# Spreading the first units' reciprocals with TensorE, taking the first block pair by pair, and zero products in planned gaps, in a fused attention and two-layer kernel

## The chip, the cores and the metric

The kernel runs on one core of a Trainium2 chip. The metric is the device time of one execution in microseconds (us).

## What is computed

Causal-by-block attention over 4 batches and 8 heads of 576 tokens with 64 columns, then two dense layers of 512 to 2048 to 512 with a nonlinearity in the middle of each. All of it is float32, on 2304 tokens.

```python
scores = scale * q @ k.T, masked where block_i < block_j (blocks of 64)
attn = exp(scores - max); attn = attn / (sum(attn) + 1e-9); x = attn @ v
h = x @ w_in;  g = h if h >= 1, 0 if h <= -1, else (h + 1) ** 2 / 4;  x = g @ w_out
h = x @ w_in2; g = max(0.01 * h, h);                                  out = g @ w_out2
```

## The kernel before

**Who orders the work.** The code builds a list of operations, each with an engine, a planned cost in ns, a priority and what it reads and writes (`Plan.op`, line 163). `Plan.schedule` (line 276) plays that list on a model of the engines forward and backward with random shifts (`SEED, TRIES = 13, 42`, line 64), keeps the order that ends first, and issues every engine's instructions in it. On the chip each engine then works in that order, so an instruction that waits holds up all that stand behind it on its engine. The model takes `port=True` operations of VectorE and GpSimd one at a time.

**Attention.** A unit is a pair of heads and a part of the rows: part "a" has chunks 0 to 2 (320 rows), part "b" chunks 3 and 4 (256 rows). There are 16 pairs, so 32 units. `unit_scores` (line 516) loads q and k, scales q on GpSimd (line 547), zeroes the columns that pad a chunk to a multiple of 128 keys (line 606, GpSimd, six a unit in part "a", four in part "b"), and multiplies into a PSUM slot (line 586). `softmax` (line 472) takes the maximum (line 484, VectorE), the exponential with its sum (line 491, ScalarE), the sum plus 1e-9 (line 495), its reciprocal (line 497), and multiplies the probabilities by it on GpSimd (line 502, one instruction a chunk and head, so six in a unit "a"). `unit_values` (line 662) transposes the probabilities (line 680), copies them out of PSUM (lines 685 and 687), and multiplies by v (line 696); in the first four units, which are parts "a" of pairs 0 to 3, 256 of the 320 columns go into the first block's input `x[0]` and `x[1]` (lines 707 and 708, the high part and the rest), the other 64 through line 710 to DRAM (line 711, queue SP). The units live in five "rooms" of SBUF (line 510).

**PSUM.** Slots 0, 3, 1 and 2 are two banks each. For the first seven units the ring of slots is 0, 3, 1, 2, and from then on 0, 3, 1 (lines 1182 to 1184). Slot 2's banks 4 and 5 go to the first layer after that: block 0 has bank 4 alone, blocks 1 and on have 4 and 5 (lines 1185 and 1202).

**Weights.** `w_float` (line 414) turns the 64-bit words of 16 slices of the first matrix into a high and a low part: a load (line 430, SP), line 431 (ScalarE), line 432 (GpSimd), lines 434 and 439 (VectorE), line 442 (ScalarE), line 445 (VectorE or GpSimd by turns).

**First layer.** `h1_block` (line 744) takes 256 tokens a block, nine blocks. Each of eight pairs of slices has two halves of three times four products of 128x128 by 128x256 (line 756), one TensorE operation of the plan for each four, and wants the whole of `x[0]` or `x[1]`; then lines 762 and 766 (ScalarE) and 767 (VectorE) empty the bank. After the attention come the conversions of the other matrices, and the layers of line 1127 and line 943, which fill TensorE to the end.

**Start.** Ten products of a zero tile (line 466) run before the first scores, into slot 2.

Of the kernel before, what the change touches and what calls it, by code (L numbers as in the profile page):

```python
# [49 lines left out]

AHEAD = 45.0


# [9 lines left out]

SEED, TRIES = 13, 42

# [87 lines left out]
class Plan:  # L153
# [122 lines left out]
    def schedule(self):  # L276
# [19 lines left out]
        for o, start, end in zip(self.ops, *best[1:]):  # L296
            o.start, o.end = start, end

        for o in done:
            o.fn()  # L300

# [3 lines left out]
def fused_kernel(ctx, tc, qk, qk2, v, w1, w2, out):  # L305
# [44 lines left out]
    def pool(cols, prio, fn, r, w, fixed=161):  # L350
        plan.op("POOL", fixed + 0.95 * cols, prio, fn, r, w, fixed != 200)

# [27 lines left out]
    ps_d.evicts.append(ps_b)  # L380
    ps_c = psum("psr", "psr", "ps_c", (), ((2, True),), "right")
    ps_e = psum("psr", "psr", "ps_e", ("psr",), ((2, False),), "right")

# [6 lines left out]
    def slot(i):  # L390

        return Bank(plan, (2 * i, 2 * i + 1), lambda: slots[i], {1: ps_b, 2: ps_c}.get(i, ps_a))

# [20 lines left out]
    def w_float(prio, fc):  # L414
# [12 lines left out]
        def upper():  # L427
# [43 lines left out]

    def softmax(prio, tag, s, parts):


        n = sum(len(p[2]) for p in parts)
        nm, sm, rs = small("nm", f"nm{tag}"), small("sm", f"sm{tag}"), small("rs", f"rs{tag}")
        i = 0
# [10 lines left out]
        for c, _, heads, view, probs, pbufs in parts:  # L488
            keys = CH[c][2]
            for k in range(len(heads)):  # L490
# [3 lines left out]
                i += 1  # L494
        act(n, prio, lambda: nc.scalar.activation(rs.get()[:, 0:n], sm.get()[:, 0:n], AF.Copy, bias=1e-9), [sm], [rs], sb=True,
            extra=60)
        dve(8, prio, lambda: nc.vector.reciprocal(rs.get()[:, 0:n], rs.get()[:, 0:n]), [rs], [rs])
# [10 lines left out]
    PCOL = {0: 0, 1: 128, 2: 384, 3: 0, 4: 512}  # L508
    units = {}
    ROOMS = {0: {"p": [(P1, 0)], "v": (P2, 1536), "qk": (P2, 2560)},  # L510
             1: {"p": [(P2, 0)], "v": (P2, 2176), "qk": (P2, 3392)},
# [4 lines left out]
    def unit_scores(pair, part, prio, ring, room_):  # L516
# [16 lines left out]
        qk_room = qs, qo, nqk  # L533
        units[pair, part] = vt, pr, prob

# [64 lines left out]
        for c in ((0, 1, 2) if part == "a" else (3, 4)):  # L600
            keys = CH[c][2]
            a, b_ = PCOL[c] + keys, PCOL[c] + (keys + 127) // 128 * 128
            for hd in range(2):
                if a == b_:
                    continue
                pool(0, prio - 1, lambda a=a, b_=b_, hd=hd: nc.gpsimd.memset(prob(hd, a, b_), 0.0), [], [part_of(hd, a, b_)], fixed=200)

# [7 lines left out]
        for grp in groups:  # L615
# [3 lines left out]
            def f(grp=grp, s=s):  # L619
                for i, (c, o) in enumerate(grp):  # L620
# [4 lines left out]
                (c, o, (0, 1), lambda s=s, o=o, c=c: s.get()[:, :, o:o + CH[c][2]],  # L625
                 [probs(c, 0), probs(c, 1)], [pbuf(c, 0), pbuf(c, 1)]) for c, o in grp])
        if part == "b":
# [10 lines left out]
            for hd in range(2):  # L638
                if ss:
                    s = ss[hd]  # L640
                else:
                    s = slot(ring[0])

                    def f(hd=hd, s=s):
# [4 lines left out]
                    (4, 224, (hd,), lambda s=s: flat2(s)[:, 224:800].rearrange("p (h k) -> p h k", h=1),  # L649
                     [probs(4, hd)], [pbuf(4, hd)])])  # L650

# [10 lines left out]
    def unit_values(pair, part, prio, ring, evac):  # L662
        n = f"{part}{pair}"
        vt, pr, prob = units[pair, part]
        pts = []
        for i, blocks in enumerate(TILES[part]):
# [7 lines left out]
            def f(blocks=blocks, s=s):  # L674
                for hd in range(2):
                    o = 0
                    for c, j in blocks:
# [21 lines left out]
        pe(sum(x[3] for x in SUMS[part]) * 1.7 + 150, prio, f, [vt] + pts, [s])  # L699
        xp = P2.reg(turn("xp", (4032, 4352)), SA)  # L700
        b, kc = divmod(pair, NKC)
        c0 = b * S + (0 if part == "a" else SA)

        q0 = 256 if c0 == 0 else 0
        if q0:
# [487 lines left out]
    for i in range(NBLK):  # L1193
# [108 lines left out]
```

## Time and profile before

| | us |
|---|---|
| three runs, median (lowest to highest) | 947.88 (946.68 to 949.87) |
| the profiled execution, its own time | 946.55 |
| its span, first to last instruction | 944.8 |
| TensorE busy in the span (98%) | 924.5 |
| VectorE, ScalarE, GpSimd busy | 759.3, 537.9, 321.2 |

Read it from TensorE: it is busy for all but 20.3 us of the span, so what can go is looked for in the stretches in which it waits. In the rows of stretches the columns are the stretch, its length, the busy time of TensorE (PE), its weight loads (PEld), VectorE (DVE), ScalarE (ACT) and GpSimd (POOL) with the number of instructions, the granted clock of TensorE as a share of full, the DMA engines' share, and GB/s.

### The profile page before, as it was taken

How to read it: one execution, taken by the hardware profiler on the slowest of the kernel's cores; microseconds unless marked ns; L12 is line 12 of the kernel's file. 1: busy time of each engine (PE TensorE's matmuls, PEld its weight loads, DVE VectorE, ACT ScalarE, POOL GpSimd, SP SyncE). 2: the span in 40 equal slices, each digit the busy share in tenths (PEclk: the TensorE clock that was granted, in tenths of full speed). 3: DMA queues.
4: the chain of work that ended last, by engine and by line, in shares of the span. 5: the costliest groups of instructions: out<-in, count | busy, mean ns of one | idle time of the engine just before them, and what ended most of it. 6: DMA issues, size and time to landing. Idle time of an engine off the chain costs nothing.

```text
span 944.8 us, 19895 instructions
## 1 busy us (share of the span) xinstructions
PE 924.5 (98%) x7324; PEld 876.0 (93%) x7324; DVE 759.3 (80%) x1289; ACT 537.9 (57%) x1060; POOL 321.2 (34%) x626
## 2 busy tenths in 40 slices
PE   7799999999999999999999999999999999999998
PEld 5467888888889999999999999999999999999998
DVE  4988867877889765779979697678888899887967
ACT  5888777877879666663334343344535563333422
POOL 6997767677665831000000020236653000000000
PEclk8999999999999999999999999999999999999999
DMA  8767878895879789976434599978885983453433
GB/s 278 235 197 224 269 255 284 297 303 185 277 264 325 262 313 326 332 246 206 149 104 143 155 348 326 342 251 276 298 292 195 322 263 91 156 156 102 145 90 113
DMA packets 168130, 221.91 MB, mean 235 GB/s; under 512 B 10080, under 2 KB 141664, under 8 KB 168032
## 3 DMA queue, kind: packets, MB, share of 16 engines
q1 hardware_dynamic: 168032, 220.63, 72.0%
q8 instruction: 58, 0.95, 0.4%
q14 instruction: 40, 0.33, 0.1%
HBM read 139.85 MB, written 80.74 MB: 233 GB/s over the span
## 4 chain that ended last, share of the span: by engine, by line
PE 91%; DVE 3%; issue 1%; ACT 1%; DMA 1%; POOL 1%; SPq 0%; DVEq 0%; ACTq 0%
PE bank L1127 30%; PE bank L756 22%; PE bank L943 18%; PE bank L1066 6%; PE slot L680 5%; PE slot L696 5%; PE slot L586 2%; PE slot L590 2%; DMA w<-w 1%; ACT rp L491 1%; DVE ra L851 1%; POOL rp L502 1%; DVE ra L1086 0%; DVE rp L687 0%; DVE wraw L1115 0%
## 5 line engine op out<-in xcount | busy, mean ns | idle before, releaser
L756 PE MATMUL bank<-ra,w 128*128 128x256 f32 x1728 | 229.2, 286 | 1.0 <-DVE rg L767 1.0
L756 PEld LDWEIGHTS bank<-ra,w 128*128 128x128 f32 x1728 | 213.2, 189 | 10.1 <-issue 5.6
L943 PE MATMUL bank<-rp,w 128*128 128x288 f32 x1344 | 180.9, 296 | 0.2 <-DVE rp L883 0.2
L943 PEld LDWEIGHTS bank<-rp,w 128*128 128x128 f32 x1344 | 179.5, 189 | 0.9 <-DVE rp L883 0.4
L851 DVE TENSOR_TENSOR ra<-ra,bank 128x288 f32<-128x288 f32 (+2 forms) x280 | 126.3, 488 | 39.9 <-ACT ra L853 13.2
L1127 PE MATMUL bank<-w,rp 128*128 128x256 f32 x1014 | 148.6, 281 | 0.0
L1127 PEld LDWEIGHTS bank<-w,rp 128*128 128x128 f32 x1014 | 132.8, 188 | 0.0
L1112 ACT ACTIVATE rp<-ra 128x1024 fp32r<-128x1024 f32 (+1 forms) x48 | 47.3, 988 | 75.7 <-DVE ra L1086 71.4
L811 POOL TENSOR_TENSOR w<-w 128x128 f32<-128x128 f32 x128 | 65.6, 533 | 41.9 <-DVE w L807 40.5
L1127 PE MATMUL bank<-rp,w 128*128 128x256 f32 x508 | 76.8, 282 | 0.0
L947 ACT ACTIVATE ra<-ra 128x1152 f32<-128x1152 f32 x32 | 37.4, 1168 | 68.0 <-DVE ra L851 68.0
L767 DVE SCALAR_TENSOR_TENSOR rg<-bank,rg 128x512 f32<-128x512 f32 x72 | 49.3, 685 | 28.5 <-ACT rg L766 28.2
L1127 PEld LDWEIGHTS bank<-rp,w 128*128 128x128 f32 x508 | 67.5, 188 | 0.1
L762 ACT ACTIVATE rg<-bank 128x512 f32<-128x512 f32 x72 | 43.0, 598 | 33.0 <-PE bank L756 32.5
L878 POOL TENSOR_TENSOR xs<-xs,rp 128x576 f32<-128x576 f32 x1 | 1.5, 1500 | 175.3 <-DMA xs<-x2d 175.3
L1115 DVE TENSOR_TENSOR wraw<-ra,rp 128x1024 fp32r<-128x1024 f32 (+1 forms) x48 | 54.3, 1134 | 6.9 <-PE bank L1127 2.4
L1127 PE MATMUL bank<-w,wraw 128*128 128x256 f32 x294 | 58.7, 282 | 0.2 <-DVE wraw L1115 0.2
L1086 DVE TENSOR_TENSOR ra<-rp,ra 128x256 f32<-128x256 f32 (+2 forms) x102 | 44.4, 439 | 2.3
L1127 PE MATMUL bank<-rg,w 128*128 128x256 f32 x280 | 46.3, 282 | 0.0
L766 ACT ACTIVATE rg<-rg 128x512 f32<-128x512 f32 x72 | 45.5, 632 | 1.0
L1086 DVE TENSOR_TENSOR ra<-rp 128x512 f32<-128x512 f32 (+2 forms) x51 | 34.4, 676 | 14.5 <-DMA rp<-gd 13.5
L1127 PEld LDWEIGHTS bank<-w,wraw 128*128 128x128 f32 x294 | 45.0, 188 | 0.6 <-DVE wraw L1115 0.4
(170 smaller groups left out, 1840.4 us busy)
## 6 DMA issues: line engine op xcount, KB each, us to landing
rp<-gd SPq DMA_DIRECT2D x41, 512.0 KB, 4.2
wcd<-w SPq DMA_DIRECT2D x43, 448.0 KB, 5.2
gd<-ra SPq DMA_DIRECT2D x32, 576.0 KB, 4.6
gd<-rg SPq DMA_DIRECT2D x64, 256.0 KB, 4.0
w<-wcd SPq DMA_DIRECT2D x32, 512.0 KB, 6.8
w<-wcd SPq DMA_DIRECT2D x32, 384.0 KB, 6.2
w<-w SPq DMA_DIRECT2D x44, 256.0 KB, 5.2
w<-w SPq DMA_DIRECT2D x16, 512.0 KB, 4.7
```

Of the source, the lines that this page charges most:

```text
L680: nc.tensor.transpose(s.get()[:, hd, o:o + 128], prob(hd, a, a + 128), ident.get())
L696: nc.tensor.matmul(s.get()[64 * hd:64 * hd + 64, 0, q0:q0 + m], lhsT=vt.get()[:, j, 64 * hd:64 * hd + 64], rhs=pts[i].get()[:, hd, o:o + m ...
L756: nc.tensor.matmul(ps.get()[:, 256 - j * 256:512 - j * 256], lhsT=win(fc, c, kc), rhs=xt[x].get()[:, kc], start=(k == 0 and kc == 0 and j ...
L767: dve(512, pv, lambda ps=ps, gt=gt: nc.vector.scalar_tensor_tensor(gt.get(), ps.get(), 1.0, gt.get(), op0=ALU.max, op1=ALU.min), [ps, gt], ...
L811: plan.op("POOL", 430, prio, lambda o=o, a=a, b=b, op=op: nc.gpsimd.tensor_tensor(sl(o), sl(a), sl(b), op=op), [(fx, (a, a + 1)), (fx, (b, ...
L851: dve(cols, prio, lambda: nc.vector.tensor_tensor(out(o), out(a), P[b][1](), op=op), [P[b][0], (slots, (a, a + 1))], [(slots, (o, o + 1))])
L943: nc.tensor.matmul(ps.get()[:, 0:HALF], lhsT=wc(1, p, cw, li, 128 * kc, 128 * kc + 128), rhs=r.get()[:, cx, kc], start=(k == 0 and kc == 0 ...
L1066: nc.tensor.matmul(ps[t].get()[:, 0:n], lhsT=wc(z, p, cw, li, 128 * t, 128 * t + 128), rhs=x.get()[:, n * zi:n * zi + n], start=(p == 0 an ...
L1086: dve(cols, pv, lambda f=f: nc.vector.tensor_tensor(*f(), op=ALU.subtract), r, [(tt, w)], port=True)
L1112: act(4 * n, pv, lambda tt=tt, ht=ht: nc.scalar.activation(s_(ht, 0, 4), s_(tt, 0, 4), AF.Copy), [tt], [ht], sb=True)
L1115: dve(4 * n, pv, lambda tt=tt, ht=ht, lt=lt: nc.vector.tensor_tensor(s_(lt, 0, 4), s_(tt, 0, 4), bc(s_(ht, 0, 4)), op=ALU.subtract), [tt, ...
L1127: nc.tensor.matmul(ps.get()[:, 256 * t:256 * t + w], lhsT=b if wide else g, rhs=g if wide else b, start=(p == 0 and k == 0 and t == 0), st ...
```

## The change

Each of these is in the diff below, cut to its core. The four first units keep their probabilities unnormalised: their reciprocals go into a tile `late` of 128x6, TensorE spreads each column over 64 partitions by a product with the identity matrix (six products a unit, float32), ScalarE copies the 320 columns to SBUF, and VectorE multiplies the values by them. ScalarE and VectorE then make `x[0]` and `x[1]` from SBUF, not PSUM. The first two pairs of block 0 are planned as one operation of three products for each quarter of the input. Pads are zeroed only where a room changes part. Slot 2 is no longer in the attention's ring; its banks 4 and 5 go to the first layer from block 0 on. The ten zero products at the start write bank 4. Where the plan has TensorE idle over 600 ns before its 20,000th ns, zero products are issued there, one for each 213 ns of 0.7 of the gap. Planned costs and port flags are changed in a few places, and the order is searched with another seed and 260 tries, so the order of all instructions is a new one.

```diff
+LATE = 4
+EARLY = 2
...
-SEED, TRIES = 13, 42
+FILL_UNTIL, FILL_SHARE = 20000, 0.7
+
+SEED, TRIES = 15, 260
...
+        last = 0
         for o in done:
+            if o.eng == "PE":
+                if last and o.start < FILL_UNTIL and o.start - last > 600:
+                    for _ in range(int((o.start - last) * FILL_SHARE / 213)):
+                        self.fill()
+                last = o.end
             o.fn()
...
-    ps_c = psum("psr", "psr", "ps_c", (), ((2, True),), "right")
-    ps_e = psum("psr", "psr", "ps_e", ("psr",), ((2, False),), "right")
+    ps_e = psum("psr", "psr", "ps_e", (), ((2, False),), "right")
...
-            op0=ALU.logical_shift_left, op1=ALU.bitwise_or), [hs, sg], [dst])
+            op0=ALU.logical_shift_left, op1=ALU.bitwise_or), [hs, sg], [dst], port=True)
...
-            dve(512, prio, low, *rw)
+            dve(512, prio, low, *rw, port=True)
...
-    zp = slot(2)
+    zp = bank(4)
+
+    def zeros():
+        nc.tensor.matmul(zp.get()[:, 0:128], lhsT=wz.get(), rhs=wz.get(), start=True, stop=True)
+    plan.fill = zeros
     for i in range(N_WARM):
-        pe(427, -1000, lambda: nc.tensor.matmul(zp.get()[:, 0, 0:128], lhsT=wz.get(), rhs=wz.get(), start=True, stop=True), [wz], [zp])
+        pe(427, -1000, zeros, [wz], [zp])
...
+        act(n, prio, lambda: nc.scalar.activation(r(), sm.get()[:, 0:n], AF.Copy, bias=1e-9), [sm], mine, sb=True, extra=60)
+        dve(8, prio, lambda: nc.vector.reciprocal(r(), r()), mine, mine)
+        if late is not None:
+            return
...
+        late = pt(st, [128, 6], F32, "late", f"late{n}", 6) if len(units) < LATE else None
...
-                if a == b_:
+                if a == b_ or padded.get(room_) == part:
                     continue
...
+        padded[room_] = part
...
-            pe(2 * m * 0.95, prio, f, [*dict.fromkeys(pr), ident], [s])
+            pe(2 * m * 0.85, prio, f, [*dict.fromkeys(pr), ident], [s])
...
+        xp = P2.reg(turn("xp", (4032, 4352)), SA)
+        if late is not None:
+            def f():
+                for i, c in enumerate((0, 1, 2) if part == "a" else (3, 4)):
+                    r = CH[c][1]
+                    q = CH[c][0] - (0 if part == "a" else SA)
+                    for hd in range(2):
+                        nc.tensor.matmul(s.get()[64 * hd:64 * hd + 64, 1, q:q + r], lhsT=late.get()[0:r, 2 * i + hd:2 * i + hd + 1].to_broadcast([r, 64]),
+                                         rhs=ident.get()[0:r, 0:r], start=True, stop=True, skip_group_check=True)
+            pe(nq * 1.7 + 150, prio, f, [ident, late], [s])
+            act(nq, prio, lambda: nc.scalar.activation(xp.get()[:, 0:nq], s.get()[:, 1, 0:nq], AF.Copy), [s], [xp])
...
+        if late is not None:
+            dve(nq, prio, lambda: nc.vector.tensor_tensor(xp.get()[:, 0:nq], s.get()[:, 0, 0:nq], xp.get()[:, 0:nq], op=ALU.mult), [s, xp], [xp])
+            if q0:
+                x = XB[0]
+                act(q0, prio, lambda: nc.scalar.activation(x[0].get()[:, kc], xp.get()[:, 0:q0], AF.Copy), [xp], [(x[0], (kc, kc + 1))], sb=True)
+                dve(q0, prio, lambda: nc.vector.tensor_tensor(
+                    x[1].get()[:, kc], xp.get()[:, 0:q0], bc(x[0].get()[:, kc]), op=ALU.subtract), [xp, (x[0], (kc, kc + 1))],
+                    [(x[1], (kc, kc + 1))], port=True)
+            dma(128 * (nq - q0) * 4, prio, lambda: nc.sync.dma_start(x1d[:, kc, c0 + q0:c0 + nq], xp.get()[:, q0:nq]), [xp],
+                [(f"x1d{kc}", (c0 + q0, c0 + nq))])
+            return
...
-            for j in range(2):
+            for kc in range(NKC if i == 0 and p < EARLY else 0):
+                for j in range(2):
+                    def f(fc=2 * p + j, j=j, kc=kc, ps=ps):
+                        for k, (c, x) in enumerate(((0, 0), (1, 0), (0, 1))):
+                            nc.tensor.matmul(ps.get()[:, 256 - j * 256:512 - j * 256], lhsT=win(fc, c, kc),
+                                             rhs=xt[x].get()[:, kc], start=(k == 0 and kc == 0 and j == 0),
+                                             stop=(k == 2 and kc == NKC - 1), skip_group_check=True)
+                    pe(3 * 119.5, pr - 8 * (NKC - 1 - kc) + 0.01 * j, f, [(W[p], (j, j + 1)), (W[p], (2 + j, 3 + j))]
+                       + [(x, (kc, kc + 1)) for x in xt], [ps])
+            for j in range(0 if i == 0 and p < EARLY else 2):
...
-    ring.append(2)
     attention(seq[:7])
-    ring.remove(2)
-    hb = [4]
+    hb = [4, 5]
...
-        if i == 1:
-            hb = [4, 5]
```

## Rows read from the trace of the kernel before

**Rows 1.** Stretches: us, busy PE, PEld, DVE, ACT, POOL, then clock, DMA.
```profile
0.00:7.40 7.40, 6.35 (x44) 5.60 (x44) 1.54 (x6) 1.80 (x5) 3.34 (x27) 1.00 0.69 209
7.40:12.70 5.30, 0.03 (x2) 0.02 (x1) 3.85 (x10) 4.45 (x22) 2.30 (x4) 0.84 1.02 339
12.70:50.00 37.30, 31.51 (x219) 19.85 (x220) 30.95 (x67) 29.58 (x102) 34.07 (x78) 0.93 0.75 250
50.00:150.00 100.00, 95.95 (x780) 80.86 (x781) 83.24 (x160) 79.85 (x221) 76.90 (x160) 1.00 0.78 242
150.00:930.00 780.00, 779.64 (x6198) 759.23 (x6197) 630.60 (x1028) 419.09 (x709) 204.63 (x361) 1.00 0.73 236
930.00:944.80 14.80, 11.06 (x89) 10.50 (x88) 9.14 (x23) 3.11 (x6) 0.00 (x0) 1.00 0.16 55
```

**Rows 2.** TensorE in order of time: start, length, line, count, idle before.
```profile
1.05 4.00 PE L466 MATMUL slot<-wz 128*128 128x128 f32 x20 [1.05 <-DVE wz L463]
4.98 2.44 PE L586 MATMUL slot<-rp 64*128 64x64 f32 x24
12.71 1.44 PE L586 MATMUL slot<-w 64*128 64x64 f32 x8 [5.29 <-ACT rp L491]
14.08 3.18 PE L680 MATMUL slot<-ident,rp 128*128 128x128 f32 x12
17.19 1.13 PE L586 MATMUL slot<-w 64*128 64x320 f32 x4
...
23.23 1.41 PE L696 MATMUL slot<-rp,rp 128*64 128x320 f32 x12
...
39.17 1.31 PE L680 MATMUL slot<-ident,rp 128*128 128x128 f32 x10 [0.48 <-ACT rp L491]
...
49.87 1.21 PE L756 MATMUL bank<-ra,w 128*128 128x256 f32 x8
...
60.55 0.73 PE L756 MATMUL bank<-ra,w 128*128 128x256 f32 x4 [1.04 <-DVE rg L767]
...
65.60 0.82 PE L586 MATMUL slot<-rp 64*128 64x64 f32 x8
...
68.27 0.81 PE L586 MATMUL slot<-rp 64*128 64x320 f32 x4 [1.05 <-DVE rp L687]
```

**Rows 3.** ScalarE: unit 0's last exponential, a weight's first pass.
```profile
9.07 0.54 ACT L491 ACTIVATE rp<-slot,nma 128x320 f32<-128x320 f32 x1
...
10.56 0.66 ACT L431 ACTIVATE xs<-w 128x512 f32<-128x512 f32 x1 [0.85 <-DMA w<-w]
```

**Rows 4.** GpSimd: reciprocals times probabilities, units 0 and 3.
```profile
11.35 3.46 POOL L502 TENSOR_SCALAR rp<-rp,rsa 64x64 f32<-64x64 f32 x6
...
28.76 2.85 POOL L502 TENSOR_SCALAR rp<-rp,rsa 64x64 f32<-64x64 f32 x6 [1.11 <-DVE rsa L497]
```

**Rows 5.** One stretch of two microseconds, columns as in rows 1.
```profile
12.00:14.00 2.00, 1.28 (x8) 0.96 (x8) 0.81 (x2) 2.00 (x11) 2.00 (x5) 0.50 1.04 420
```

**Rows 6.** TensorE's waits, first 60 us: total, times, longest.
```profile
PE slot L586 <- ACT rp L491: 6.2, 3, 5.3
PE slot L680 <- POOL rp L502: 2.2, 3, 1.0
```

**Rows 7.** 30 to 50 us, columns as in rows 1.
```profile
30.00:50.00 20.00, 15.86 (x121) 9.73 (x118) 18.79 (x39) 16.82 (x53) 19.43 (x36) 1.00 0.72 229
```

**Rows 8.** Line 708 on VectorE: ns shortest, median, longest; first and last start.
```profile
L708 DVE TENSOR_TENSOR ra<-slot,ra x4: 416/424/425, 20.7 to 38.3; 128x256 fp32r<-128x256 f32 x4
```

**Rows 9.** Line 606, the pads, whole run, columns as in rows 8.
```profile
L606 POOL MEMSET rp<- x98: 144/152/156, 1.2 to 296.0; 128x64 f32 x98
L606 POOL MEMSET w<- x62: 142/152/159, 2.3 to 309.0; 128x64 f32 x62
```

**Rows 10.** Groups by line, first 60 us: count, busy us, mean ns.
```profile
L434 DVE SCALAR_TENSOR_TENSOR w<-w 128x512 int32<-128x512 int32 x10 | 8.2, 817 | 1.4 <-POOL w L432 1.4
```

**Rows 11.** Line 434 alone, columns as in rows 8.
```profile
L434 DVE SCALAR_TENSOR_TENSOR w<-w x10: 661/688/1170, 11.3 to 56.9; 128x512 int32<-128x512 int32 x10
```

More of the change, by code (lines that the diff above doesn't have):

```diff
@@ L350, in pool @@
     def pool(cols, prio, fn, r, w, fixed=161):
-        plan.op("POOL", fixed + 0.95 * cols, prio, fn, r, w, fixed != 200)
+        plan.op("POOL", fixed + 0.95 * cols, prio, fn, r, w, fixed != 86)
     def dma(nbytes, prio, fn, r, w):
@@ L390, in slot @@
     def slot(i):
-        return Bank(plan, (2 * i, 2 * i + 1), lambda: slots[i], {1: ps_b, 2: ps_c}.get(i, ps_a))
+        return Bank(plan, (2 * i, 2 * i + 1), lambda: slots[i], {1: ps_b}.get(i, ps_a))
     def bank(i):
@@ L463, in fused_kernel, with softmax @@
     dve(0, -100, lambda: nc.vector.memset(wz.get(), 0.0), [], [wz], fixed=200)
-    zp = slot(2)
+    zp = bank(4)
+    def zeros():
+        nc.tensor.matmul(zp.get()[:, 0:128], lhsT=wz.get(), rhs=wz.get(), start=True, stop=True)
+    plan.fill = zeros
     for i in range(N_WARM):
-        pe(427, -1000, lambda: nc.tensor.matmul(zp.get()[:, 0, 0:128], lhsT=wz.get(), rhs=wz.get(), start=True, stop=True), [wz], [zp])
+        pe(427, -1000, zeros, [wz], [zp])
     dummy = Buf(plan, "dummy", 1, lambda: const.tile([128, 8], F32, name="dummy"))
     act(8, -1000, lambda: nc.scalar.activation(dummy.get(), wz.get()[:, 0:8], AF.Exp), [wz], [dummy], extra=1280)
-    def softmax(prio, tag, s, parts):
+    def softmax(prio, tag, s, parts, late=None):
         n = sum(len(p[2]) for p in parts)
-        nm, sm, rs = small("nm", f"nm{tag}"), small("sm", f"sm{tag}"), small("rs", f"rs{tag}")
+        nm, sm = small("nm", f"nm{tag}"), small("sm", f"sm{tag}")
         i = 0
@@ L494, in softmax, with r @@
                 i += 1
-        act(n, prio, lambda: nc.scalar.activation(rs.get()[:, 0:n], sm.get()[:, 0:n], AF.Copy, bias=1e-9), [sm], [rs], sb=True,
-            extra=60)
-        dve(8, prio, lambda: nc.vector.reciprocal(rs.get()[:, 0:n], rs.get()[:, 0:n]), [rs], [rs])
+        e = 0
+        if late is not None:
+            e = 2 * parts[0][0] + parts[0][2][0]
+            e -= 6 * (e > 5)
+            rs = late
+        else:
+            rs = small("rs", f"rs{tag}")
+        mine = [(rs, (e, e + n))]
+        def r():
+            return rs.get()[:, e:e + n]
+        act(n, prio, lambda: nc.scalar.activation(r(), sm.get()[:, 0:n], AF.Copy, bias=1e-9), [sm], mine, sb=True, extra=60)
+        dve(8, prio, lambda: nc.vector.reciprocal(r(), r()), mine, mine)
+        if late is not None:
+            return
         i = 0
@@ L509, in fused_kernel @@
     units = {}
+    padded = {}
     ROOMS = {0: {"p": [(P1, 0)], "v": (P2, 1536), "qk": (P2, 2560)},
@@ L533, in unit_scores @@
         qk_room = qs, qo, nqk
-        units[pair, part] = vt, pr, prob
+        late = pt(st, [128, 6], F32, "late", f"late{n}", 6) if len(units) < LATE else None
+        units[pair, part] = vt, pr, prob, late
         q0, k0, nq, nk, nj = (SA, 0, SA, SA, 3) if part == "a" else (0, SB, SB, S, 5)
@@ L603, in unit_scores @@
             for hd in range(2):
-                if a == b_:
+                if a == b_ or padded.get(room_) == part:
                     continue
-                pool(0, prio - 1, lambda a=a, b_=b_, hd=hd: nc.gpsimd.memset(prob(hd, a, b_), 0.0), [], [part_of(hd, a, b_)], fixed=200)
+                pool(0, prio - 1, lambda a=a, b_=b_, hd=hd: nc.gpsimd.memset(prob(hd, a, b_), 0.0), [], [part_of(hd, a, b_)], fixed=86)
+        padded[room_] = part
         def pbuf(c, hd):
@@ L625, in unit_scores @@
                 (c, o, (0, 1), lambda s=s, o=o, c=c: s.get()[:, :, o:o + CH[c][2]],
-                 [probs(c, 0), probs(c, 1)], [pbuf(c, 0), pbuf(c, 1)]) for c, o in grp])
+                 [probs(c, 0), probs(c, 1)], [pbuf(c, 0), pbuf(c, 1)]) for c, o in grp], late)
         if part == "b":
@@ L649, in unit_scores @@
                     (4, 224, (hd,), lambda s=s: flat2(s)[:, 224:800].rearrange("p (h k) -> p h k", h=1),
-                     [probs(4, hd)], [pbuf(4, hd)])])
+                     [probs(4, hd)], [pbuf(4, hd)])], late)
     def flat2(s):
@@ L663, in unit_values @@
         n = f"{part}{pair}"
-        vt, pr, prob = units[pair, part]
+        vt, pr, prob, late = units[pair, part]
         pts = []
@@ L698, in f @@
                                      skip_group_check=True)
-        pe(sum(x[3] for x in SUMS[part]) * 1.7 + 150, prio, f, [vt] + pts, [s])
-        xp = P2.reg(turn("xp", (4032, 4352)), SA)
+        pe(sum(x[3] for x in SUMS[part]) * 1.7 + 230, prio, f, [vt] + pts, [s])
         b, kc = divmod(pair, NKC)
@@ L704, in unit_values @@
         q0 = 256 if c0 == 0 else 0
+        if late is not None:
+            dve(nq, prio, lambda: nc.vector.tensor_tensor(xp.get()[:, 0:nq], s.get()[:, 0, 0:nq], xp.get()[:, 0:nq], op=ALU.mult), [s, xp], [xp])
[8 more added lines that the diff above has]
+            return
         if q0:
```

## The prediction

> **What bounds the kernel now.** I first cut the span into stretches and read TensorE's busy time in each [rows 1]. From 150 to 930 us it is idle for 0.36 us of 780: there the kernel is TensorE's own work, and the change leaves that work as it is. The loss is ahead of it: 5.27 of the 5.30 us from 7.4 to 12.7, 5.79 of the next 37.3, and 4.05 between 50 and 150. The last 14.8 us lose 3.74 in the closing sums and stores, which the change doesn't touch. So a gain can come only from the first 150 us, and any of it counts in full, as TensorE has no slack behind.
>
> In TensorE's order of time [rows 2] the reader sees how the start goes: zero products to 5.05 us, the scores of units 0 and 1 to 7.42, nothing for 5.29 us, and then the scores of unit 2 and the transposes of unit 0. ScalarE and GpSimd tell why: unit 0's last exponential begins at 9.07 us [rows 3], yet GpSimd multiplies its probabilities from 11.35 for 3.46 us [rows 4], and the transposes stand behind that. ScalarE itself sat 0.85 us before line 431, whose load had not landed, with unit 1's exponentials queued behind it. After the pause TensorE's granted clock is 0.50 [rows 5], the lower of its levels (1.2 of 2.4 GHz). The waits of the first 60 us name the same two sources: exponentials 6.2 us, GpSimd's multiplications 2.2 [rows 6]. From 30 to 50 us GpSimd is busy 19.43 of 20 us, VectorE 18.79, ScalarE 16.82, TensorE 15.86 [rows 7]: four engines close together, with GpSimd in front.
>
> **The change part by part**, against the profiled execution's own 946.55 us. It lies 1.33 under the median of the three runs, 947.88; I add half of that, 0.65, to each sum to speak of a median.
>
> *The clock.* If TensorE does not stand still as long, work of 12.7 to 18.3 us runs at the upper level. Eight score products took 1.44 us there and 0.82 at 65.60; four took 1.13 and 0.81 at 68.27; twelve transposes took 3.18, and ten took 1.31 at 39.17, so twelve 1.57, but some 0.5 us of the 3.18 was waiting [rows 2]. That is 0.62 + 0.32 + 1.1 = 2.0. I take -2.0. The other end is 0: the zero products stand where the plan has a gap, and the chip's gap may be elsewhere.
>
> *The first gap.* With the reciprocals taken after the values, unit 0's transposes need only its exponentials, done by about 9.7 us [rows 3], not 14.08. The third slot goes to unit 1's first scores, and its second ones now wait for a slot of unit 0, so some 0.8 us of scores move into the gap. Left empty are about 2.3 of 5.3 us if all follows at once, but ScalarE has unit 1's exponentials, weights and evictions to do in the same time. I take -2.5, between 0 and -4.0.
>
> *GpSimd's multiplications.* Four units times six go. Unit 0's took 3.46, unit 3's 2.85 [rows 4], the others lie near; about 12 us of GpSimd's 34.07 between 12.7 and 50 [rows 1]. That brings it from 91% to about 60% there, and it stops being in front. The weights' steps of lines 432 and 445, queued behind these, come earlier. VectorE is next, with 30.95 of 37.3 [rows 1], and it gets more (below). TensorE's idle 5.79 us in this stretch shrink. The first two pairs' 48 products, quarter by quarter, are work for the holes: four products took about 0.6 us at 49.87 to 51.08 [rows 2], so 48 are some 7 us that can stand where TensorE waited, as long as slices 0 to 3 of the weights are ready. I take -3.0, between 0 and -5.8 (all of it).
>
> *The spreading.* Six products a unit are new on TensorE. The nearest row is line 696's: twelve took 1.41 us for 1408 columns [rows 2], these have 640, so 0.64; by the transposes' 0.131 each it is 0.79. I take 0.7, four times, +2.8, counted in full although some stands in holes (0 to +3.2). ScalarE gets a 320-column copy a unit, four in all, and VectorE a product of 320 columns: line 708 took 0.424 for 256 [rows 8], so 0.53, together 2.1 us. They lie between the values and `x[0]`. Unit 3's subtraction began at 38.3 [rows 8] and block 0's first product at 49.87 [rows 2], so a delay of a microsecond there is covered by 11 us; were pairs 0 and 1 to take up `x` at once, it would cost up to 0.5 a unit, which the -3.0 allows for. The store of line 711 now waits for VectorE's product, with v and weight loads queued behind it on SP; they are shifted by that half microsecond and are issued ahead of their use: 0 to +0.5, taken as 0. The subtraction reads two SBUF operands now and may stand behind a GpSimd instruction: at most 3.46 / 6 = 0.58 each [rows 4], on VectorE, off TensorE's path.
>
> *Pads.* 160 of 0.15 us go [rows 9] down to 36 by the order of rooms in the code: 18.6 us of GpSimd over 310 us, never a release named in [rows 6]; 0, or a little inside the -3.0.
>
> *Two banks for block 0.* TensorE waited 1.04 us at 60.55 for line 767 to empty the only bank [rows 2]. I take -1.0, and -0.5 of the other 3 us from 50 to 150, where GpSimd and VectorE run lighter: -1.5, between 0 and -4.05.
>
> *The lost slot.* With three slots in the ring TensorE waited 1.05 us at 68.27 for one to be emptied [rows 2]. For the seven first units I take +0.5, since exponentials are late there in any case; the other end is 7 x 1.05 = +7.4.
>
> *Zero products.* Each holds TensorE, in order. Ten took 4.00 us at the start [rows 2], 0.4 each, against the 0.213 by which they are counted. By that a planned gap would be filled 1.3 times over: 0.3 of 5.3 us is +1.6. At the upper clock they should be shorter. I take +0.3, between 0 and +1.6.
>
> *The new order.* From 150 us on there is 0.36 us to gain and no row that shows what another order would lose; 0, with -0.3 to +2.
>
> Sum: -2.0 - 2.5 - 3.0 + 2.8 - 1.5 + 0.5 + 0.3 = -5.4, so 941.15, and 941.8 as a median.
>
> **A rule weighed.** Line 434 on VectorE took 0.817 us on average [rows 10] and 0.661 at its shortest [rows 11]: ten of them gave away 1.6 us. That may be GpSimd's doing, and would shrink with its load. The Trainium skill (SBUF — State Buffer, SBUF: two separate sides) says that VectorE, when it reads two SBUF operands, and GpSimd lock a common pair of ports, and the loser waits for the whole instruction. The rows bear it out in part: the longest took 1.170 [rows 11], but the median, 0.688, is next to the shortest. By the rule alone the sum would be up to 1.6 us lower, 940.2; against the change, it also covers the new subtraction.
>
> **The rivals.**
> 1. *The holes close* (936.5). GpSimd was the one cause, everything behind it moves up: -2.0 - 4.0 - 5.0 + 2.8 - 2.5 = -10.7, so 935.85, 936.5 as a median. For it: GpSimd at 19.43 of 20 [rows 7]. Against: three other engines close behind.
> 2. *The zeros miss* (943.8). The change doesn't keep the clock up, since the chip's gap isn't the plan's: the same sum without the 2.0. For it: the plan did not know of the late load at line 431 [rows 3].
> 3. *VectorE takes over* (945.8). It is at 18.79 of 20 [rows 7] and gets 2.1 us more; the chain gains nothing from a freer GpSimd: -2.0 - 1.5 - 1.0 + 2.8 + 0.3 = -1.4, so 945.15, 945.8 as a median.
> 4. *Slots bind* (951.0, slower). In order, TensorE stands before line 586 until a slot is empty, one such wait of 1.05 us a unit, half of the 7.4 us where it was idle anyway. The idle of before stays: -2.0 - 1.0 + 2.8 + 0.3 + 3.7 = +3.8, so 950.35, 951.0 as a median. It is slower than what can be told from no change once the new waits pass 3.4 us, three to four units' worth.
>
> **How the numbers follow.** A measurement of this kernel can tell about 0.3%, 2.8 us, so faster means under 945.0 and slower over 950.7. Forecast 0.45; rivals 1 to 4: 0.15, 0.10, 0.17, 0.13. Forecast, rival 1 and 0.07 of rival 2 are faster: 0.67. Rival 3 less 0.01 and the rest of rival 2 are the same: 0.19. Rival 4 and that 0.01 are slower: 0.14. The forecast's own range is 938 to 945. The range of 8 in 10 cuts rival 1 in half at 936.0 and leaves out half of rival 4 at 950.0.
>
> **What would show it.** Right: no stretch with a clock of 0.50 after the start; unit 0's transposes near 10 us; GpSimd under 70% from 12.7 to 50; block 0's products among the first units' before 45 us; idle of TensorE from 12.7 to 50 near 3 us, and no wait for line 767 in block 0. Wrong: a sum of waits at line 586 over 3 us behind 12.7 (rival 4); VectorE over 95% from 12.7 on with TensorE as idle as before (rival 3); a pause with the clock at 0.50 behind it (rival 2); or idle of over a microsecond between 150 and 930, which no row of before foresees.

## The result, and the profile after

The changed kernel takes 936.73 us in the median of four runs (933.62 to 940.52), the kernel before 947.28 beside it (946.3 to 949.87): a ratio of 0.9886 [0.9841, 0.9932], so 10.6 us or 1.1% faster. The forecast was 941.8 us, the range 936.0 to 950.0: the sign is right, the time lies near the range's low end and outside the forecast's own 938 to 945, and the gain is 1.7 times the 6.1 us forecast. It is the number of rival 1 (936.5), but, as the runs below show, not by rival 1's way.

The stretches of the changed kernel, to be laid beside [rows 1, 5, 7], with the same columns:

```profile
0.00:7.40 7.40, 6.35 (x41) 5.85 (x42) 1.18 (x4) 1.49 (x2) 3.51 (x27) 1.00 0.67 208
7.40:12.70 5.30, 4.79 (x40) 3.95 (x42) 3.62 (x9) 4.71 (x23) 1.71 (x4) 1.00 1.01 365
12.00:14.00 2.00, 1.86 (x20) 1.28 (x18) 2.00 (x5) 1.50 (x10) 0.67 (x2) 1.00 1.02 411
12.70:50.00 37.30, 35.04 (x286) 24.26 (x283) 33.71 (x74) 31.35 (x98) 24.09 (x38) 1.00 0.77 255
30.00:50.00 20.00, 19.25 (x150) 13.93 (x149) 17.18 (x38) 16.01 (x47) 15.89 (x20) 1.00 0.63 200
50.00:150.00 100.00, 97.02 (x778) 79.94 (x780) 81.03 (x160) 82.50 (x232) 69.31 (x111) 0.98 0.75 238
150.00:930.00 780.00, 776.38 (x6220) 755.07 (x6217) 635.52 (x1040) 417.60 (x706) 205.73 (x302) 1.00 0.73 237
930.00:938.70 8.70, 4.96 (x41) 4.57 (x39) 3.98 (x10) 1.02 (x2) 0.00 (x0) 0.90 0.16 60
```

TensorE's idle time up to 150 us is 1.05 + 0.51 + 2.26 + 2.98 = 6.8 us; before it was 1.05 + 5.27 + 5.79 + 4.05 = 16.2 [rows 1]. The start is repaired, by 9.4 us of idle. GpSimd falls from 34.07 to 24.09 us of the 37.3. The reader should then stop at the row from 150 to 930: TensorE is idle for 3.62 us there, before for 0.36, and yet it did 22 more products in the same 780 us (6220 against 6198). Busy time says nothing of that.

TensorE in order of time in the changed kernel, beside [rows 2]:

```profile
5.39 1.91 PE L613 MATMUL slot<-rp 64*128 64x64 f32 x20
7.22 1.83 PE L476 MATMUL bank<-wz 128*128 128x128 f32 x14
9.57 0.81 PE L613 MATMUL slot<-rp 64*128 64x320 f32 x4 [0.51 <-ACT rp L504]
10.31 0.88 PE L709 MATMUL slot<-ident,rp 128*128 128x128 f32 x6
11.02 0.61 PE L476 MATMUL bank<-wz 128*128 128x128 f32 x4
...
13.88 0.92 PE L728 MATMUL slot<-ident,latea 64*64 64x64 f32 x12
...
22.71 0.97 PE L805 MATMUL bank<-ra,w 128*128 128x256 f32 x6
...
53.20 1.44 PE L613 MATMUL slot<-rp 64*128 64x320 f32 x4 [1.54 <-DVE rp L716]
```

Unit 0's transposes begin at 10.31 us where they began at 14.08, zero products (line 476) stand in the planned gaps, and block 0's first products run from 22.71, not from 49.87. The price of the spreading, from the groups of the first 60 us (line 728 on TensorE has a second form of the same kind, line 731 is the copy, line 745 the multiplication):

```profile
L745 DVE TENSOR_TENSOR rp<-slot,rp 128x320 f32<-128x320 f32 x4 | 1.9, 486 | 0.6 <-ACT rsa L519 0.6
...
L731 ACT ACTIVATE rp<-slot 128x320 f32<-128x320 f32 x4 | 1.7, 435 | 0.3 <-PE slot L728 0.3
...
L728 PE MATMUL slot<-ident,latea 128*64 128x128 f32 x32 | 2.6, 285 | 0.0
...
L728 PE MATMUL slot<-ident,latea 64*64 64x64 f32 x16 | 1.3, 242 | 0.3
```

And the waits of TensorE over the whole run, in total, times, longest:

```profile
PE bank L1186 <- DVE rp L1172: 1.6, 1, 1.6
PE slot L613 <- DVE rp L716: 1.5, 1, 1.5
PE bank L1002 <- DVE ra L910: 1.2, 2, 0.8
...
PE bank L815 <- DVE rg L826: 0.5, 1, 0.5
```

The profiled execution took 940.52 us, its span is 938.7, 6.1 us shorter than before. Weighing each product by its usual length, I worked out from the two traces how much earlier the same amount of TensorE's work is done in the changed kernel: 3.5 us earlier at 140 us, 6.0 at the end. So the start gave 3.5 of the 6.1 us in this execution, the slowest of the four, and 2.6 came behind it, where I had said that nothing could come.

### The profile page after: what moved, and what is told of

It reads as the page before. It is cut to its first block, busy times and chain, and to the rows that moved or that the text cites. A ratio compares the mean times of both kernels' runs of the same rounds, so it can differ in the third digit from the quotient of the medians.

```text
span 938.7 us, 19954 instructions
## 1 busy us (share of the span) xinstructions
PE 924.5 (98%) x7394; PEld 873.6 (93%) x7394; DVE 759.0 (81%) x1293; ACT 538.7 (57%) x1060; POOL 304.3 (32%) x478
## 4 chain that ended last, share of the span: by engine, by line
PE 88%; DVE 4%; DMA 3%; issue 2%; ACT 1%; POOL 0%; SPq 0%; DVEq 0%; ACTq 0%
PE bank L1186 29%; PE bank L815 21%; PE bank L1002 15%; PE bank L1125 6%; PE slot L736 6%; PE slot L709 5%; PE slot L613 3%; PE slot L617 2%; DMA gd<-ra 1%; DVE ra L910 1%; DMA wcd<-rg 1%; DVE ra L1145 1%; DMA w<-w 1%; PE bank L805 1%; DMA wraw<-w 0%
## 5 line engine op out<-in xcount | busy, mean ns | idle before, releaser
L815 PE MATMUL bank<-ra,w 128*128 128x256 f32 x1680 | 224.7, 284 | 0.5 <-DVE rg L826 0.5
L815 PEld LDWEIGHTS bank<-ra,w 128*128 128x128 f32 x1680 | 206.5, 188 | 8.6 <-issue 6.4
L870 POOL TENSOR_TENSOR w<-w 128x128 f32<-128x128 f32 x128 | 69.2, 564 | 18.1 <-DVE w L866 16.4
L1186 PE MATMUL bank<-rg,w 128*128 128x256 f32 x280 | 48.4, 280 | 0.0
L1145 DVE TENSOR_TENSOR ra<-rp,ra 128x256 f32<-128x256 f32 (+2 forms) x102 | 41.9, 418 | 2.4 <-DMA x2d<-ra 0.2
```

Source lines behind the costliest of these rows:

```text
L815: nc.tensor.matmul(ps.get()[:, 256 - j * 256:512 - j * 256], lhsT=win(fc, c, kc), rhs=xt[x].get()[:, kc], start=(k == 0 and kc == 0 and j ...
L870: plan.op("POOL", 430, prio, lambda o=o, a=a, b=b, op=op: nc.gpsimd.tensor_tensor(sl(o), sl(a), sl(b), op=op), [(fx, (a, a + 1)), (fx, (b, ...
L1145: dve(cols, pv, lambda f=f: nc.vector.tensor_tensor(*f(), op=ALU.subtract), r, [(tt, w)], port=True)
L1186: nc.tensor.matmul(ps.get()[:, 256 * t:256 * t + w], lhsT=b if wide else g, rhs=g if wide else b, start=(p == 0 and k == 0 and t == 0), st ...
```

## The experiments

Ratios are to the kernel before on the same chip, with a 95% interval. Each run has one traced execution, which need not lie at the run's median.

**The change's parts.** First the changed kernel once more, for the same chips as its variants.

> The changed kernel once more, beside the kernel before. Theory A (the start): its first 107 us are 4 to 5 us shorter in every run, and the ratio lies near 0.989 to 0.994. Theory N (part of the gain was the chip of the first comparison, whose four runs of the changed kernel lay 6.9 us apart): the ratio is nearer to 1 than 0.995, or the runs lie as far apart again, in two groups by whether the clock falls behind a pause at 51 us.

Measured: 935.66 us (934.97 to 937.74) against 947.36, 0.9886 [0.987, 0.9901]. The result stands; the gain is a little larger than the 0.989 to 0.994 of theory A.

**Without the zero products** in the gaps, in the same order:

```diff
-FILL_UNTIL, FILL_SHARE = 20000, 0.7
+FILL_UNTIL, FILL_SHARE = 20000, 0.0
```

> The changed kernel and its very order, without the 11 zero products in the gaps. Theory C (the zero products keep the clock): TensorE stands still from 7.3 to about 9.3 us and for two short holes, the clock falls to 0.50 somewhere between 9 and 18 us, and the time rises by 1 to 3 us over the changed kernel. Theory A: unit 0's transposes come at 10.3 us either way, no pause is longer than 2.3 us, so the clock stays up without the zeros and the time moves by less than 0.7 us.

Measured: 938.57 us (936.32 to 941.78), 0.9918 [0.9899, 0.9938]. In its profile the clock stayed at 1.00 through a pause of 2.3 us at the start and fell first near 53 us. The medians lie 2.9 us apart and the intervals just touch, so the zeros are worth something between nothing and some 5 us. Whether they are worth it by the clock stays open: the traced execution is the fastest of the six, and the two slowest, 941.76 and 941.78 us, have a mean granted clock of 0.993 and 0.990 over the execution, the other four 0.996 to 0.998. No trace of those two shows where it fell.

**Without the spreading** (the reciprocals multiplied on GpSimd as before, all else as changed, the order searched anew):

```diff
-LATE = 4
+LATE = 0
```

> The changed kernel with GpSimd multiplying the first four units' probabilities again (no spreading), and an order searched anew in the same way. Theory A: 3 to 6 us of the gain go, so the ratio to the kernel before is 0.995 to 0.999, with GpSimd over 85% busy from 12.7 to 50 us. Theory B (the new search gives the gain): the ratio stays within 0.002 of the changed kernel's, 0.987 to 0.992.

Measured: 945.58 us (941.32 to 947.61), 0.9975 [0.996, 0.999]. Nearly the whole gain is gone. That looked like proof that the spreading carries it. It is not: without spreading there is no tile `late` either, and below the place of the tiles behind it proves to count for most. Nor does it show that the spreading is worth nothing, as the new order has other products closer together late in the run (see the place of the operands).

**The order alone**, the kernel before with the new seed and tries:

```diff
-SEED, TRIES = 13, 42
+SEED, TRIES = 15, 260
```

> The kernel before with the new seed and 260 tries alone. Theory B: it keeps most of the gain, a ratio of 0.990 to 0.994. Theory A: 0.997 to 1.003, since GpSimd's chain, the four slots, the single bank of block 0 and the pause of 5 us are all there still.

Measured: 953.26 us (950.01 to 955.1), 1.0069 [1.0052, 1.0086]: slower. TensorE's waits in its profile:

```profile
PE slot L586 <- POOL rp L502: 5.7, 1, 5.7
PE slot L586 <- ACT rp L685: 3.8, 3, 2.4
```

A longer search alone put first scores behind GpSimd's multiplications for 5.7 us. The plan's end is not the chip's, and a new order is worth several us either way.

**The clock by itself.** The kernel before, in its own order, with zero products into columns that nobody reads:

```diff
+        last = 0
         for o in done:
+            if o.eng == "PE":
+                if last and o.start < 20000 and o.start - last > 600:
+                    for _ in range(int((o.start - last) * 0.7 / 213)):
+                        self.fill()
+                last = o.end
             o.fn()
...
+    plan.fill = lambda: nc.tensor.matmul(slots[0][:, 1, 384:512], lhsT=wz.get(), rhs=wz.get(), start=True, stop=True)
```

> The kernel before in its very order, with zero products in the planned gaps of its first 20 us (into columns that nothing reads). Theory C: the clock's lower stretch from 11.1 to 17.9 us goes, and the time falls by about 2 us, a ratio of 0.998. If the pause of 5.3 us itself were the loss, nothing moves: 0.9995 to 1.001.

Measured: 946.32 us against 946.66, 0.9999 [0.9986, 1.0011]. Its stretches:

```profile
12.00:14.00 2.00, 1.46 (x14) 1.26 (x15) 1.08 (x3) 2.00 (x10) 2.00 (x4) 1.00 1.05 426
...
12.70:50.00 37.30, 31.25 (x237) 20.12 (x237) 32.45 (x69) 29.70 (x103) 34.77 (x82) 1.00 0.73 250
```

The granted clock is 1.00 where it was 0.50 [rows 5], and nothing is gained: TensorE still is idle for 6.05 us from 12.7 to 50, as it was for 5.79. Its products ran at the upper level and then waited for ScalarE and GpSimd.

The same question for the dip that the changed kernel has near 53 us (0.83 granted from 50 to 60): its order, with seven zero products in the planned gap there. The changed kernel's stretch first:

```profile
50.00:60.00 10.00, 8.43 (x59) 6.09 (x60) 7.79 (x17) 9.24 (x29) 7.36 (x12) 0.83 0.58 202
```

```diff
+                if last and 50000 < o.start < 54000 and o.start - last > 600:
+                    for _ in range(int((o.start - last) * FILL_SHARE / 213)):
+                        self.fill2()
```

> The changed kernel in its very order, with 7 zero products more, in the planned gap near 50 us (into columns that nothing reads). Theory C: the clock, which fell to 0.50 at 53 us for 3.4 to 6.8 us in the profiles of the changed kernel, stays up, and the time falls by 1.5 to 3.5 us under the changed kernel's, a ratio to the kernel before of 0.985 to 0.987. Rival: the stretch at half clock lies beside waits for VectorE, and nothing is gained: 0.988 to 0.990.

Measured: 937.86 us (935.9 to 938.76), 0.9904 [0.9891, 0.9917].

```profile
50.00:60.00 10.00, 8.46 (x72) 6.88 (x71) 7.55 (x16) 8.95 (x30) 7.10 (x12) 1.00 0.47 146
```

The clock stays up, and no gain shows against the changed kernel's 0.9886 from other chips.

**GpSimd's multiplications.** The changed kernel in its own order, with the 24 multiplications put back behind the exponentials, by 1.0 (so their values change nothing): once in place, so that the transposes wait for them, and once into a tile `aside` that nobody reads, so that only GpSimd has them to do. The diff is of the first; in the second the output is `aside`.

```diff
+                    if late is not None:
+                        r_ = CH[c][1]
+                        nc.gpsimd.tensor_scalar(probs[k]()[0:r_], probs[k]()[0:r_], 1.0, 1.0, op0=ALU.mult, op1=ALU.mult)
```

> The changed kernel in its very order, with GpSimd's 24 multiplications back, by 1.0, on the first four units' probabilities, each right behind its exponential and so ahead of the transposes. Theory A (the transposes no longer wait for GpSimd): 4 to 8 us of the gain go, a ratio of 0.993 to 0.997, with waits for these multiplications ahead of the transposes. If the gain were the spreading of other work (blocks by quarters, banks, order): under 1.5 us go.

> The same 24 multiplications, written to a tile that nobody reads: GpSimd has the load, TensorE does not wait for it. Theory A1 (the wait is what cost): under 1.5 us go, a ratio of 0.989 to 0.990. Theory A2 (GpSimd's load cost, through the weights' steps queued behind): as much goes as in the run in place, 0.993 to 0.997.

Measured: in place 938.53 us (935.67 to 941.71), 0.9908 [0.989, 0.9927]; aside 940.18 us (937.33 to 944.21), 0.9934 [0.9914, 0.9954]. The stretch from 12.7 to 50 us, in place:

```profile
12.70:50.00 37.30, 33.49 (x277) 23.18 (x276) 33.82 (x70) 29.46 (x94) 32.06 (x56) 1.00 0.74 245
```

GpSimd is back at 32.06 us, TensorE's idle time rises from 2.26 to 3.81, and the kernel loses some 2 us against the ratio of the changed kernel (0.9886, from another chip), or 4.5 aside; against the order with seven zeros on the same chip (0.9904) it is 0.4 and 2.8. Either way most of the 10.6 us stays. The loss was expected larger in place, at 4 to 8 us, and came smaller there than aside. Whether the wait or the load costs more isn't told apart: the two kernels also differ by how closely TensorE's products follow each other late in the run, the subject of the next experiments. And `aside` is no neutral tile: its 1,280 bytes lie in the pool `const`, ahead of all others, so that it moves the weights and the operands alike.

**The place of the operands.** What the runs so far have in common: a gain of 0.7 to 1.1% wherever the tiles `late` are there, and hardly any where they are not. These tiles take 192 bytes of each partition (six buffers of 24 bytes, 32 bytes apart), in a pool that lies ahead of the pool `rm`. In `rm` lie the tiles that TensorE multiplies in the layers (`ra`, `rg`, `rp`), so the whole pool moves on by 192 bytes. Two kernels cross order and place. The first is the kernel before, with 192 unused bytes ahead of `rm`:

```diff
+    pad = ctx.enter_context(tc.tile_pool(name="pad", bufs=1))
+    pad.tile([128, 48], F32, tag="pad", name="pad")
     rm = ctx.enter_context(tc.tile_pool(name="rm", bufs=1))
```

> The kernel before in its very order, with an unused tile of 192 bytes a partition ahead of the pool that holds the moving operands, so that they lie where the changed kernel has them. Theory P (where the operands lie sets the pace of the long stretch): products of 256 columns from 460 us on go from 118.7 and 120.0 ns apart to 117.8 and 113.3, and the time falls by 2 to 6 us, a ratio of 0.994 to 0.998. Theory Q (the pace comes from the order and its pauses): 118.7 and 120.0 ns as in the kernel before, a ratio of 0.999 to 1.001.

The second is the changed kernel, with `late` in a pool behind `rm`, so that this pool begins where it began before:

```diff
     rm = ctx.enter_context(tc.tile_pool(name="rm", bufs=1))
+    lt = ctx.enter_context(tc.tile_pool(name="lt", bufs=1))
...
-        late = pt(st, [128, 6], F32, "late", f"late{n}", 6) if len(units) < LATE else None
+        late = pt(lt, [128, 6], F32, "late", f"late{n}", 6) if len(units) < LATE else None
```

> The changed kernel in its very order, with the tiles of the spread reciprocals behind that pool, so that the moving operands lie where the kernel before has them. Theory P: the products go back to 118.7 and 120.0 ns, and 3 to 6 us of the gain go, a ratio of 0.992 to 0.995. Theory Q: 117.8 and 113.3 ns, a ratio of 0.987 to 0.990.

And two more places, with the pad of the first diff in the changed kernel, of 72 and of 32 numbers (288 and 128 bytes more):

> The changed kernel in its very order, with 288 bytes more ahead of that pool, so that the moving operands begin at multiples of 512 bytes. Theory P: another pace than 113.3, 117.8, 118.7 or 120.0 ns may come up, faster or slower, and the time moves by over 2 us. Theory Q: 117.8 and 113.3 ns, a ratio of 0.987 to 0.990.

> The changed kernel in its very order, with 128 bytes more ahead of that pool. If the pace repeats with the place every 128 bytes, products lie 117.8 and 113.3 ns apart and the ratio is 0.987 to 0.990, as in the changed kernel. If it does not, another pace comes up: back to 118.7 or 120.0 ns (0.995 to 1.000), or one that holds 113.3 for longer, and the ratio falls under 0.985.

| order | `rm` moved by | us | ratio |
|---|---|---|---|
| before | 0 | 947.0 | 1 |
| before | 192 bytes | 940.1 (935.0 to 941.08) | 0.9922 [0.9903, 0.9941] |
| changed | 0 | 943.95 (942.02 to 944.71) | 0.9969 [0.9957, 0.998] |
| changed | 192 bytes | 935.66 (934.97 to 937.74) | 0.9886 [0.987, 0.9901] |
| changed | 480 bytes | 946.61 (943.02 to 947.98) | 0.9995 [0.9984, 1.0006] |
| changed | 320 bytes | 933.76 (930.88 to 935.41) | 0.9852 [0.9828, 0.9877] |

The rows of 935.66 and 933.76 us are from another chip than the rest; the ratios hold for each. 192 bytes that nobody uses make the kernel before 0.8% faster, with every instruction as it was. Both pairs move by more than theory P had expected: 0.9922 for 0.994 to 0.998, and 0.9969 for 0.992 to 0.995. Without the shift, the change's own work is worth 0.3%. The two add up: 0.9922 times 0.9969 is 0.9891, and the changed kernel has 0.9886. Another place takes all of it back, another gives more: the last row is the fastest of all, 14.1 us under the kernel before on its chip.

The trace shows where the time goes. A stretch in which TensorE only works, 800 to 860 us, with 150 to 930 above it. The kernel before (its row from 150 to 930 is in [rows 1]):

```profile
800.00:860.00 60.00, 60.00 (x508) 60.00 (x508) 51.20 (x74) 24.22 (x27) 0.00 (x0) 1.00 0.47 141
```

The kernel before, moved by 192 bytes:

```profile
150.00:930.00 780.00, 778.12 (x6290) 757.00 (x6288) 638.46 (x1052) 422.55 (x716) 205.66 (x360) 1.00 0.72 236
800.00:860.00 60.00, 60.00 (x532) 60.00 (x531) 50.82 (x73) 24.68 (x27) 0.00 (x0) 1.00 0.45 130
```

The changed kernel, not moved:

```profile
150.00:930.00 780.00, 779.43 (x6197) 759.63 (x6197) 632.66 (x1036) 416.43 (x701) 202.90 (x301) 1.00 0.72 237
800.00:860.00 60.00, 60.00 (x508) 60.00 (x508) 52.30 (x75) 25.02 (x27) 0.00 (x0) 1.00 0.47 146
```

The changed kernel, moved by 480 bytes:

```profile
150.00:930.00 780.00, 777.90 (x6168) 757.05 (x6167) 630.20 (x1025) 415.85 (x703) 205.00 (x304) 1.00 0.72 236
800.00:860.00 60.00, 60.00 (x513) 60.00 (x513) 53.10 (x75) 24.04 (x26) 0.00 (x0) 1.00 0.46 143
```

Busy time is 60.00 us of 60 in all four, the clock is 1.00 in all, and the products done are 508, 532, 508 and 513. Over 780 us they are 6198, 6290, 6197 and 6168: in these 60 us of the last layer the fourth is no slower than the kernel before, so its loss lies elsewhere. The moved kernel before does 92 products more in 780 us, at 0.12 us each some 11 us of work. Its traced execution took 935.0 us, the shortest of its six; by the median, 940.1, the gain is some 7 us. The last layer's largest group of products shows the same as a length: shortest, median and longest in ns, then first and last start. Before:

```profile
L1127 PE MATMUL bank<-w,rp x1014: 274/281/318, 760.5 to 940.9; 128*128 128x256 f32 x169
```

Before, moved by 192 bytes:

```profile
L1129 PE MATMUL bank<-w,rp x1014: 276/276/362, 754.7 to 929.3; 128*128 128x256 f32 x169
```

The changed kernel, not moved:

```profile
L1187 PE MATMUL bank<-w,rp x1014: 274/281/387, 756.4 to 936.1; 128*128 128x256 f32 x169
```

The changed kernel, moved by 320 bytes:

```profile
L1188 PE MATMUL bank<-w,rp x1014: 276/279/388, 747.8 to 927.0; 128*128 128x256 f32 x169
```

The layer takes 180.4, 174.6, 179.7 and 179.2 us. The moved kernel before gains 5.8 us inside this one layer. The unmoved changed kernel enters it 4.1 us ahead of the kernel before and leaves it 4.8 ahead: what it has, it has from the start. The one moved by 320 bytes had its gain earlier: it enters 12.7 us ahead.

The place is not alone in this. From 620 to 720 us TensorE works on products of 288 columns (line 943). The kernel before, and the one with the new order alone, whose operands lie where they lay before:

```profile
620.00:720.00 100.00, 100.00 (x753) 100.00 (x752) 81.65 (x168) 47.57 (x70) 50.45 (x74) 1.00 0.79 263
```

```profile
620.00:720.00 100.00, 100.00 (x772) 100.00 (x771) 82.63 (x172) 47.70 (x69) 57.52 (x78) 1.00 0.83 278
```

These products start 133.3 ns apart in the first and 130.0 in the second, and 130.0 in the kernel without spreading too: 3.3 ns on 1344 products, an estimate of 4.4 us that both orders gained there without a shift. So the order alone lost more elsewhere than its ratio says, and by that estimate the kernel without spreading would be at 950.0 us without them (945.58 + 4.4), slower than the 947.36 before. What a new order and a new place do are thus told apart only by pairs of one order, which the table has.

## Why the prediction was right or wrong

**The step that failed** is a sentence at the head of it: that from 150 to 930 us "the change leaves that work as it is", so that "a gain can come only from the first 150 us", and the 0 that I set for the new order there. It rested on a busy share of 779.64 in 780 [rows 1]. Such a share leaves no room for more waiting to vanish, but it doesn't say how far apart the products start. In the kernel before neighbouring products of 256 columns mostly start 118.7 ns apart; in those moved by 192 and 320 bytes 113.3 or 117.8; in the one moved by 480 bytes 117.3 to 120.0 (each a mean over successive starts in a stretch without a pause). The change moved the operands, by tiles of 24 bytes a partition that I read in the diff and priced at nothing, as it cost no time of any engine. That is worth 0.8%, about 7 us of the 10.6. That the time still fell inside the range is luck: the larger part of the gain came from a thing that the sum doesn't have.

The Trainium skill (Trainium Kernel Development and Optimization, Performance Expectations) calls TensorE's busy time a bad metric for how close a kernel is to its roofline, as matmuls are pipelined. The rows agree: 60.00 us of 60 with 508 products and with 532. Had I weighed that sentence, [rows 1] would not have closed the long stretch.

**The start** was seen rightly, but its worth was put too high. Without the shift the change gives 3.0 us (943.95 against 947.0), where I summed 5.4; the difference lies in what the terms are worth in time, as most of the signs of the start came. Term by term:

- *The clock, -2.0*: the reason came true, the gain did not. Up to 50 us no stretch has a clock of 0.50, and transposes run at full rate; but the kernel before with its clock held up gains nothing (0.9999). The sign "no stretch with a clock of 0.50 after the start" failed later, from 50 to 60 us, where 0.83 of full means 3.4 us at 0.50, beside the wait of 1.54 us at 53.20. I had priced busy time at two levels of the clock, while ScalarE and GpSimd, not TensorE, set when the next work came.
- *First gap, -2.5*: idle there fell from 5.27 to 0.51 us, but some 2.3 us of the stretch (the 0.61 and, from 7.40 on, 1.65 of the 1.83) are zero products, not work. The transposes are 3.8 us earlier, at the time forecast.
- *GpSimd, -3.0*: idle from 12.7 to 50 fell by 3.5 us, to 2.26 (forecast near 3), GpSimd to 65% (forecast under 70%). But the multiplications put back cost only 0.4 to 4.5 us.
- *Spreading, +2.8*: 2.6 + 1.3 us in the groups, which overlap, 3.7 together; 0.92 a unit for 0.7. The six products are twelve instructions in the trace. VectorE's product took 0.486 us for 0.53 forecast, ScalarE's copy 0.435. *Zeros, +0.3*: 22 instructions of eleven products, 3.15 us of TensorE, some 2.3 of it where it was idle before.
- *Two banks, -1.5, and lost slot, +0.5*: the wait of 1.04 us in block 0 is gone (the one wait for line 826, 0.5 us, comes after 350 us); new are 1.54 us at 53.20 us and the 0.7 of line 736, more than the 0.5 forecast. Together idle from 50 to 150 fell by 1.07 us, for 1.0 forecast, but the parts weren't tried alone, nor were the fewer pads or the pair-by-pair block.
- *Rule weighed*: 24 of GpSimd's instructions came and went with 0.4 to 4.5 us of the whole; that is no separate test of a lock between the two engines. Nor do the durations settle it: with less for GpSimd to do, line 434 (now 443) went from 0.817 us [rows 10] to 0.858 on average and line 439 (now 448) from 0.83 to 0.68, in the first 60 us. The lock stays open.

So 9.4 us of idle time went, and 3.7 us of spreading and 3.15 us of zeros took their place; the remaining 2.6 us lie next to the 3.0 that the unmoved changed kernel gains. My sum counted new work at 3.1 us, where it is 6.9, and idle at some 7, and then the clock once more.

**The rivals.** Rival 1's time came, but the holes alone don't give it: they close in the unmoved kernel too, which is at 943.95 and has 1.88 us of idle from 12.7 to 50:

```profile
12.70:50.00 37.30, 35.42 (x292) 24.77 (x290) 33.14 (x74) 31.25 (x98) 23.93 (x37) 1.00 0.76 258
```

Rival 2 is out: the clock stayed up at the start, in the traced execution without the zeros too, and holding it up in the kernel before gained nothing. Rival 3 is out: VectorE is at 33.71 of 37.3, 90%, and the idle went all the same. Rival 4 is out: 1.54 us at one slot, not 3.7.

**What would make it wrong** named idle of over a microsecond from 150 to 930. It came, 3.62 us, of which TensorE waits 1.6 us for VectorE's line 1172 and 1.2 for its line 910. In the unmoved changed kernel it is 0.57, so it came with the closer products; that they cause it is the likely reading, not a tested one.

**What stays open**: why the place bears on the spacing, and why a new order alone does. Four offsets were tried, the weights stayed where they were within one order, and no run looked at one operand alone. Between the two orders, `ra0` and a few weights also trade places in their pools, by multiples of 512 bytes; no run looked at that.

## What to carry to other kernels

A stretch in which TensorE is busy all the time isn't closed: count the products in it, and compare the count where both kernels do the same ones. A count tells of its stretch alone: the order alone did 6229 products from 150 to 930 us, 31 more than the kernel before, and is slower in the whole. Before crediting a change with a gain there, run the old order with the new tiles' bytes as an unused pad, and the new order with the new tiles behind the operands; and where a kernel lives on TensorE, a few pads, such as the 192 and 320 bytes here, are a cheap thing to try; 480 bytes took the gain back. Price a higher clock only where TensorE is what the next work waits for.

## What the runs showed of the hardware

**The place of the streamed tiles in SBUF bears on how closely products follow each other**, for the same 256 columns at a clock of 1.00: 118.7 ns, in parts up to 120.0, where the kernel before has them, 113.3 or 117.8 moved by 192 or 320 bytes, 117.3 to 120.0 moved by 480. The Trainium skill (TensorE: Matmul & The Clock Gate, Step-by-step: what each phase is for) gives TensorE two independent read ports, so that loading weights takes nothing from the running product; the rows agree in that products and weight loads are both busy 60.00 us of 60, but a pad of 192 bytes that changes the pace by up to 4.5% isn't foreseen there. By the same page (Back-to-back issue gap) 256 / 2.4 + 2.5 gives an estimate of 109.2 ns for a product taken by itself; the closest measured here is 113.3.

**In the last layer's traces the spacing holds for tens of us, and comes out otherwise, if at all, behind an interruption.** The same program in two executions (that of the result and that of the second comparison), TensorE in order of time around the first wait of the last layer. In the first:

```profile
761.12 0.39 PE L1186 MATMUL bank<-w,rp 128*128 128x256 f32 x2
761.35 0.39 PE L1186 MATMUL bank<-w,rg 128*128 128x256 f32 x2
...
767.42 0.74 PE L1186 MATMUL bank<-w,rp 128*128 128x256 f32 x4 [1.60 <-DVE rp L1172]
767.99 0.40 PE L1186 MATMUL bank<-w,rg 128*128 128x256 f32 x2
768.23 0.40 PE L1186 MATMUL bank<-w,rp 128*128 128x256 f32 x2
```

In the second:

```profile
763.03 0.40 PE L1186 MATMUL bank<-w,rg 128*128 128x256 f32 x2
763.26 0.40 PE L1186 MATMUL bank<-w,rp 128*128 128x256 f32 x2
...
767.86 0.74 PE L1186 MATMUL bank<-w,rp 128*128 128x256 f32 x4 [0.20 <-DVE rp L1172]
768.44 0.39 PE L1186 MATMUL bank<-w,rg 128*128 128x256 f32 x2
768.67 0.39 PE L1186 MATMUL bank<-w,rp 128*128 128x256 f32 x2
```

Two products take 0.39 us ahead of the wait and 0.40 behind it in the first, 0.40 ahead and 0.39 behind in the second: the pace changed from 113.3 to 117.8 ns in the one and the other way in the other, and each kept its own for some 100 us. That is an estimate of 3.8 us per 100 us, enough for the width of the changed kernel's runs, 933.62 to 940.52. What decides the draw isn't known. The clock is a rival for a part of that width: of the eight executions of the changed kernel in both comparisons, the five with a mean granted clock of 0.999 or 1.000 took 933.62 to 936.05 us, the three with 0.996 to 0.998 took 937.74 to 940.52. It can't be the whole: the six with GpSimd's multiplications in place all had 0.999 or 1.000, and took 935.67 to 941.71.
